# DeltaNet and a PReLU feed-forward on one core: the opening of the kernel put in another order

## The chip, the core and the metric

The kernel runs on one core of a Trainium2 chip. Its engines work side by side, each through its own queue of instructions in the order written: TensorE (PE, with its weight loads shown as PEld), VectorE (DVE), ScalarE (ACT), GpSimd (POOL) and SyncE (SP, which here only starts DMAs). They wait for each other by semaphores. The time is device microseconds of the whole program, as a median over runs.

## The reference

There are 4 batches of 8 heads, 768 tokens each, head dimension 48. For every head a 48x48 state goes through the tokens:

```python
k_n = k / (np.linalg.norm(k, axis=-1, keepdims=True) + 1e-06)
for t in range(S):
    y[:, :, t] = einsum('bhd,bhde->bhe', q[:, :, t], state)
    v_old = einsum('bhde,bhd->bhe', state, k_n[:, :, t])
    state = state + beta[t] * einsum('bhd,bhe->bhde', k_n[:, :, t], v[:, :, t] - v_old)
```

The 3072 outputs of 384 numbers (8 heads x 48) then go through a feed-forward: `h = x @ w_in` (384 x 2048), `g = max(h, 0) + alpha * min(h, 0)` with one alpha for each of the 2048 columns, and `g @ w_out` (2048 x 384). All is float32.

## The kernel before

**Tiling.** The recurrence is cut into 12 chunks of 64 tokens. A step is one chunk of two batches: one batch in partitions 0 to 63, the other in 64 to 127, so there are N = 24 steps and 8 heads in each. Inside a chunk the recurrence is a triangular system of 64 unknowns for each head and batch. Its matrix is the Gram matrix of the keys, weighted by beta and the keys' norms. It is inverted by blocks: 32x32 diagonal blocks first, and what lies between them by products.

**What one step needs.** `squared` squares the keys on ACT (L348). `norms` sums them on DVE (L352). `weigh` takes the root and adds the epsilon on ACT (L364, L365); its second half, `weigh_rest`, takes the reciprocal on DVE (L371), and multiplies beta and the weights by it on POOL (L373, L374). `flip` transposes the keys on PE (L384), and an ACT copy brings them to SBUF as `k_t` (L410, or L393 in `flipped`). `grams` makes the Gram matrix on PE (L436). It returns three pieces, which are called later: two DVE evictions that apply the weights (L442, into `same` and `right`), and `keep`, which copies one part of `right` into `same` on POOL (L485), DVE (L487) or ACT (L489).

**The first four steps** (NJ = 4) are inverted together, since their diagonal blocks fill the 128 lanes. `turn_in` puts the blocks one to a lane by four DVE transposes (L501). `eliminate_small` inverts the 16x16 sub-blocks on the diagonal: a product with a mask `inside` (L563), then 14 steps of two DVE instructions each (L569, L575), while POOL clears the rest of the tile (L580 to L582). `back` transposes the result into the tiles `turned` and `inverse` (L501). `cross` then joins the 16x16 blocks to 32x32 ones on PE: products of `edge` and `turned` (L605), a copy on ACT to `half_way` (L610), products with `half_way` for `turned` (L615) and for `inverse` (L622), and DVE additions of both (L629, L631). `place` puts the blocks into `diag` and `inv` (L650, L654), and `between_1` (L721) and `between_2` (L734) join them to 64x64.

**Order.** Every engine's order is written out by hand; nothing is reordered. The main body first issues all loads on SP, makes the four steps' Gram matrices in a loop, transposes the queries of steps 0 and 1 (`flips(N, i)`, copies L412), makes the products of queries and keys (`queries`, L1417), transposes alpha (`slopes`, L310, and on ACT L311 into `al_t`), clears tiles on ACT (`zeros`, L327 and L329), and calls `busy(BUSY)`: products of 128x512 that nobody reads (L1407), each shown as two records in the trace. `begin_in(4)` puts the first ACT halves of the weights' conversion on ACT's queue (L226, L227; the DVE halves are L236 and L241). Then come the elimination, `first_chunk` (steps 0 and 1 as far as the state), and `second_pair`, where steps 2 and 3 go along with the first feed-forward products (L943). From there a planner (`weave`) mixes the pieces of recurrence and feed-forward by their counts.

PSUM tiles: `ps_big` and `ps_one` go round three pairs of banks, `ps_ffn` round two single banks.

## Time and profile before

| | us |
|---|---|
| time, median of 3 runs | 661.9 (661.86 to 667.46) |
| span of the profiled execution, first to last instruction | 658.5 |
| median less span | 3.4 |
| PE busy | 642.4 (98%) |
| DVE busy | 490.4 (74%) |
| ACT busy | 263.9 (40%) |
| POOL busy | 93.4 (14%) |
| PE busy in the first 22 us | 13.7 |

The profile gives the profiled execution's span, and no other time of its own; the 3.4 us are the median's distance from that span.

How to read it: in the timeline a line has the start and the length in microseconds, engine, line of the kernel, operation, what is written and read, and how many instructions were merged. In square brackets stands the idle time of that engine just before it, and what ended that. In the chain of work that ended last each line has a start, a length, and an engine with the tile and line; "issue" is time for which the profile shows no one that was waited for. A line number can be that of a helper, which several callers share.

### The profile page before, as it was taken

To read this page: it belongs to the slowest core of one execution; us is meant where nothing else is said; L and a number is where in the kernel's file an instruction comes from. 1 tells how busy PE (TensorE), PEld (TensorE's weight loads), DVE (VectorE), ACT (ScalarE), POOL (GpSimd) and SP (SyncE) were. 2 spreads that over 40 slices of the span, in tenths; PEclk is the share of its full clock that TensorE was granted. 3 is DMA by queue.
4 is the path that set the end of the run, shared out by engine and by line. 5 is a ranking of instruction groups with operands and counts; after the bars stand their busy time and mean duration, and the time that the engine had idled before them with its cause. 6 is when DMAs were issued, how large, how long until landed. Compare 5 with 4: busy or idle time off the path is not lost.

```text
span 658.5 us, 22123 instructions
## 1 busy us (share of the span) xinstructions
PE 642.4 (98%) x9545; PEld 567.5 (86%) x9545; DVE 490.4 (74%) x1180; ACT 263.9 (40%) x621; POOL 93.4 (14%) x201
## 2 busy tenths in 40 slices
PE   5999999999999999999999999999999999999997
PEld 4477888657788988988988988988989999999997
DVE  3975899977999779658869758868868658567383
ACT  4855755344453443143253242133245245042140
POOL 6000211010000000000000000000035044052260
PEclk9999999999999999999999999999999999999999
DMA  7946745311422122122111111111111210100000
GB/s 124 293 97 158 194 121 148 73 36 37 75 54 50 34 54 38 25 59 41 26 43 33 26 39 36 26 42 33 26 44 32 45 32 2 31 8 2 24 1 25
DMA packets 111154, 37.72 MB, mean 57 GB/s; under 512 B 104224, under 2 KB 107440, under 8 KB 111056
## 3 DMA queue, kind: packets, MB, share of 16 engines
q1 hardware_dynamic: 109184, 35.81, 24.5%
q8 instruction: 75, 1.23, 0.8%
q10 hardware_dynamic: 1872, 0.49, 0.4%
q14 instruction: 23, 0.19, 0.1%
HBM read 31.56 MB, written 4.72 MB: 55 GB/s over the span
## 4 chain that ended last, share of the span: by engine, by line
PE 91%; DVE 5%; ACT 1%; issue 1%; POOL 1%; DMA 1%; SPq 0%; POOLq 0%; ACTq 0%; DVEq 0%
PE p_ffn L943 24%; PE p_ffn L1008 17%; PE p_more L1260 8%; PE p_ffn L986 5%; PE p_more L1176 5%; PE p_ffn L1166 3%; PE p_ffn L1260 3%; PE p_pair L775 2%; PE p_pair L384 2%; PE p_ffn L1171 2%; PE p_pair L686 2%; PE p_pair L800 2%; PE p_pair L813 2%; PE p_pair L1407 2%; PE p_pair L436 2%; PE p_pair L760 1%
## 5 line engine op out<-in xcount | busy, mean ns | idle before, releaser
L943 PE MATMUL p_ffn<-xt,w_in 128*128 128x256 f32 x768 | 176.1, 383 | 0.6 <-DVE act L955 0.5
L943 PEld LDWEIGHTS p_ffn<-xt,w_in 128*128 128x128 f32 x768 | 142.4, 190 | 21.2 <-issue 1.5
L955 DVE SCALAR_TENSOR_TENSOR act<-act,al_t,p_ffn 128x256 f32<-128x256 f32 x112 | 48.7, 476 | 26.5 <-ACT act L953 26.5
L953 ACT ACTIVATE act<-p_ffn 128x512 f32<-128x512 f32 x56 | 33.2, 594 | 79.4 <-PE p_ffn L943 79.2
L534 DVE TENSOR_TENSOR block<-block,prod 128x30 f32<-128x30 f32 (+9 forms) x150 | 49.8, 332 | 5.2
L1200 POOL TENSOR_TENSOR k_t<-k_t 128x128 f32<-128x128 f32 (+1 forms) x48 | 29.3, 610 | 167.1 <-ACT k_t L1195 164.6
L528 DVE TENSOR_TENSOR prod<-block 128x30 f32<-128x30 f32 (+9 forms) x150 | 48.8, 326 | 1.4
L1008 PE MATMUL p_ffn<-w_out,act 128*128 128x192 f32 x288 | 49.6, 328 | 0.0
L854 ACT COPY xt<-p_pair 128x384 f32<-128x384 f32 x22 | 10.4, 478 | 91.1 <-PE p_pair L852 77.3
L1008 PEld LDWEIGHTS p_ffn<-w_out,act 128*128 128x128 f32 x288 | 46.5, 190 | 0.3
L373 POOL TENSOR_TENSOR beta_t<-beta_t,rec 128x8 f32<-128x8 f32 x24 | 6.3, 265 | 283.9 <-DVE rec L371 268.6
L1200 POOL TENSOR_TENSOR block<-block 128x128 f32<-128x128 f32 (+1 forms) x48 | 27.9, 582 | 17.2 <-ACT block L1195 14.7
L1166 PE MATMUL p_ffn<-xt,w_in 128*128 128x256 f32 x96 | 28.7, 381 | 0.5 <-DVE o_sb L1028 0.5
L785 DVE TENSOR_TENSOR r<-v_raw,p_pair 64x192 f32<-64x192 f32 (+1 forms) x66 | 23.3, 353 | 2.3 <-PE p_pair L775 1.2
L698 ACT COPY inv<-p_pair 32x256 f32<-32x256 f32 x40 | 14.4, 361 | 25.0 <-DVE u L804 24.2
L352 DVE TENSOR_REDUCE norm<-ksq 128x8 f32<-128x384 f32 x24 | 13.0, 548 | 14.3 <-ACT ksq L348 14.3
L804 DVE TENSOR_TENSOR u<-p_pair,wgt 128x384 f32<-128x384 f32 x24 | 13.2, 556 | 14.0 <-PE p_pair L686 14.0
L1028 DVE TENSOR_TENSOR o_sb<-u,p_ffn 128x192 f32<-128x192 f32 x24 | 8.0, 352 | 20.4 <-PE p_ffn L1008 20.0
L1214 DVE SCALAR_TENSOR_TENSOR act<-block,al_t,act 128x256 f32<-128x256 f32 x32 | 19.1, 638 | 5.3 <-ACT block L1210 5.2
L764 ACT COPY y<-p_pair 128x384 f32<-128x384 f32 x22 | 10.4, 478 | 30.2 <-PE p_pair L760 26.1
L1260 PE MATMUL p_more<-w_out,act 128*128 128x192 f32 x128 | 21.8, 329 | 0.0
L1195 ACT COPY k_t<-p_more 128x512 f32<-128x512 f32 x16 | 9.4, 585 | 31.1 <-PE p_more L1176 26.4
(228 smaller groups left out, 1422.1 us busy)
## 6 DMA issues: line engine op xcount, KB each, us to landing
w_out<-in_moe_w_in_dram SPq DMA_DIRECT2D x10, 512.0 KB, 5.5
qp<-in_q_dram SPq DMA_DIRECT2D x48, 96.0 KB, 3.0
v_raw<-in_v_dram SPq DMA_DIRECT2D x48, 96.0 KB, 2.9
kl<-in_k_dram SPq DMA_DIRECT2D x96, 48.0 KB, 2.5
out_dram<-o_sb SPq DMA_DIRECT2D x90, 48.0 KB, 1.6
space_out<-in_moe_w_out_dram SPq DMA_DIRECT2D x11, 384.0 KB, 4.1
ke<-in_k_dram SPq DMA_DIRECT2D x43, 96.0 KB, 3.3
w_out<-in_moe_w_out_dram SPq DMA_DIRECT2D x5, 384.0 KB, 4.0
```

The lines of the kernel that those rows point to most:

```text
L528: nc.vector.tensor_tensor(out=prod, in0=r[:, 0:j, j : j + 1].to_broadcast([128, j, n]), in1=r[:, j : j + 1, j + 1 : HB].to_broadcast([128, ...
L534: nc.vector.tensor_tensor(out=r[:, 0:j, j + 1 : HB], in0=r[:, 0:j, j + 1 : HB], in1=prod, op=ALU.add)
L785: nc.vector.tensor_tensor(out=r[to, a], in0=v_in[to, a], in1=p[own, a, :, 0:D], op=ALU.subtract)
L943: nc.tensor.matmul(p_h[:, i], w_in[:, t, (f + i) * 128 : (f + i + 1) * 128], xt[:, t], start=(t == 0), stop=(t == KT - 1),)
L953: nc.scalar.activation(g, p_h, ACT.Relu, scale=-1.0)
L955: nc.vector.scalar_tensor_tensor(out=g[:, i], in0=g[:, i], scalar=al_t[:, f + i : f + i + 1], in1=p_h[:, i], op0=ALU.mult, op1=ALU.add,)
L986: nc.tensor.matmul(p_o[u], gs[f // 2][:, f % 2, u * 128 : (u + 1) * 128], w_out[:, f], start=(f == 0), stop=(f == FT - 1),)
L1008: nc.tensor.matmul(p, x(i), w(i), start=(i == 0), stop=(i == FP - 1))
L1166: nc.tensor.matmul(p[:, f * 256 : f * 256 + 256], w(2, f), xt[:, 2], start=True, stop=False)
L1176: nc.tensor.matmul(q[:, j], a, b, start=True, stop=True)
L1200: nc.gpsimd.tensor_tensor(out=dst, in0=a, in1=b, op=ALU.add)
L1260: nc.tensor.matmul(p, x(i), w(i), start=(i == 0), stop=(i == FP - 1))
```

## The change

The opening's order is written anew, and four things beside it are altered:

- All four steps' norms, reciprocals and weights are put ahead of the evictions of the Gram matrices as far as possible, in the queues of ACT, DVE and POOL; the POOL copies of `keep` come after the weights. For steps 2 and 3 `keep` uses DVE and ACT and no longer POOL. The transposed keys use the two single banks.
- The mask `inside` with its tile `ones` and its cast on ACT is gone. In its place 15 POOL memsets clear what lies below the diagonal.
- `slopes` comes after the queries.
- `cross` adds the products for `turned` (L629) ahead of the products for `inverse` (L622), with a `yield` between them. `first_chunk` places the first parts of `diag` in that gap, and its filler `busy(1.25)` is gone.
- `BUSY` is 6 instead of 8 (12 records instead of 16), and 6 products of the identity with itself (128x128) stand at PE's beginning.

```diff
-BUSY = 8
+BUSY = 6
+WARM = 6
...
-    ones = work.tile([128, HB, HB], FP32, name="ones", tag="turned", bufs=1)
-    nc.gpsimd.memset(ones, 0.0)
-    nc.gpsimd.affine_select(
...
@@ keep
-            if n < FIRST + NJ and n != NJ - 1:
+            if n < 2 or NJ <= n < FIRST + NJ:
                 nc.gpsimd.tensor_copy(out=same[m][own, j], in_=right[n % EARLY][own, 1:])
@@ eliminate_small
-        nc.vector.tensor_tensor(out=x, in0=x, in1=own_blocks(inside_), op=ALU.mult)
+        for j in range(1, LB):
+            nc.gpsimd.memset(x[:, :, j, 0:j], 0.0)
@@ cross
+        for i in (0, 2):
+            y = turned[m][quad(i), bs, 0:LB]
+            nc.vector.tensor_tensor(out=y, in0=y, in1=p[quad(i), 1], op=ALU.add)
+        yield
         for b in range(n):
             for i in range(4):
                 nc.tensor.matmul(
...
-        for i in (0, 2):
-            y = turned[m][quad(i), bs, 0:LB]
-            nc.vector.tensor_tensor(out=y, in0=y, in1=p[quad(i), 1], op=ALU.add)
@@ first_chunk
         next(middle)
-        busy(1.25)
         place(0, (0,))
         place(1, (0,), True)
+        next(middle)
         for i in both:
             place(i, (1,), True)
+        for i in both:
             now(between_1(i))
@@ main body
-    squares(0)
-    flips(0, N)
+    for _ in range(WARM):
+        nc.tensor.matmul(big[0][:, 0, 0:128], ident, ident)
+    squared(0)
+    norms(0)
+    now(flipped(0, ps_ffn()))
+    squared(1)
+    norms(1)
     betas()
     fetch_in(n_in + 2)
-    squares(1)
-    now(weigh(0))
-    for n in range(1, NJ):
-        if n == 1:
-            gram = grams(0)
-        flips(n, N)
-        if n > 1:
-            gram = grams(n - 1)
-        now(gram)
-        if n + 1 < NJ:
-            squares(n + 1)
-        now(weigh(n))
-        load_early(n + NKE)
-    now(grams(NJ - 1))
-    nc.scalar.copy(inside, ones)
+    rest = [weigh(0), weigh(1)]
+    gram = {0: grams(0)}
+    squared(2)
+    now(flipped(1, ps_ffn()))
+    for x in rest:
+        now(x)
+    norms(2)
+    rest = weigh(2)
+    now(flipped(2, ps_ffn()))
+    squared(3)
+    now(rest)
+    now(gram[0][:2])
+    load_early(1 + NKE)
+    gram[1] = grams(1)
+    norms(3)
+    rest = weigh(3)
+    now(flipped(3, ps_ffn()))
+    now(rest)
+    now(gram[1][:2])
+    for n in range(2, NJ):
+        load_early(n + NKE)
+        gram[n] = grams(n)
+    for n in range(2, NJ):
+        now(gram[n - 2][2:])
+        now(gram[n][:2])
+    for n in range(2, NJ):
+        now(gram[n][2:])
+    for i in range(2):
+        flips(N, i)
     edges(0, edge)
     load_late(1)
     load_v(2)
-    slopes()
-    for i in range(2):
-        flips(N, i)
     for i in range(2):
         load_q(i + 2)
     mask = queries()
+    slopes()
@@ second_pair
         next(halves[0])
+        next(halves[0])
...
         next(halves[1])
+        next(halves[1])
```

More of the change, by code (lines that the diff above doesn't have):

```diff
@@ L265 @@
         nc.gpsimd.tensor_copy(out=above[half(t)], in_=upper[half(t), half(t)])
-    ones = work.tile([128, HB, HB], FP32, name="ones", tag="turned", bufs=1)
-    nc.gpsimd.memset(ones, 0.0)
-    nc.gpsimd.affine_select(
-        out=ones, in_=ones, compare_op=ALU.is_ge, fill=1.0, base=0,
-        pattern=[[1, HB], [-1, HB]], channel_multiplier=0,
-    )
-    inside_ = const.tile([128, HB * (HB + 1)], S8, name="inside")
-    inside = inside_[:, 0 : HB * HB].rearrange("p (r c) -> p r c", c=HB)
     which = const.tile([128, 2], FP32, name="which")
@@ L438, in grams @@
             )
-        w = stats[n][1][:, 0:2, :, None].to_broadcast([128, 2, G, HB])
         def weighted(dst, cols):
+            w = stats[n][1][:, 0:2, :, None].to_broadcast([128, 2, G, HB])
             nc.vector.tensor_tensor(
```

## The prediction

> **What bounds the kernel now.** I read three views: the busy times by stretch of the span, the chain that ended last in its order of time, and the timeline of each engine up to 62 us.

> The stretches (length; busy time and count of PE, PEld, DVE, ACT, POOL; clock; DMA share; GB/s):

> ```profile
> 0.00:22.00 22.00, 13.66 (x224) 11.20 (x225) 11.51 (x35) 11.87 (x36) 10.93 (x43) 1.00 0.82 190
> 22.00:41.60 19.60, 18.97 (x416) 11.02 (x414) 15.78 (x46) 13.11 (x28) 0.00 (x0) 1.00 0.80 198
> 54.00:100.00 46.00, 45.59 (x973) 38.95 (x974) 36.82 (x97) 31.57 (x73) 8.63 (x20) 1.00 0.62 159
> ```

> After 54 us PE is never free; the longest PE waits there that name another engine are 0.5 us. So the end is about the time at which PE reaches 54 us, plus 604.5. Only the opening can move it, and a microsecond saved before 54 should be one at the end. Only 3.4 us lie outside the span (661.9 median less 658.5); I have no other own time of the profiled execution.

> The chain in the opening (start, length, what):

> ```profile
> 12.29 0.39 POOL same L485
> ...
> 13.20 0.21 POOL beta_t L373
> ...
> 16.03 0.42 DVE same L442
> 16.45 0.34 DVE right L442
> 16.81 0.41 ACT same L489
> 17.25 1.03 ACT inside L1553
> 18.29 0.62 ACT sums L589
> ...
> 19.51 1.98 PE p_ffn L1417 x57
> 21.49 9.26 PE p_pair L1407 x16
> 30.75 1.32 PE p_pair L605 x88
> ```

> GpSimd copies (L485) stand ahead of the next step's weights (L373), the cast of the mask stands ahead of the query copies, and then 16 fillers hold PE until 30.7. The timeline shows what else is late (start, length, instruction, idle before and its releaser):

> ```profile
> 15.74 0.28 PE L310 MATMUL p_pair<-ident,al_sb 16*128 16x16 f32 x1 [1.68 <-DMA al_sb<-in_moe_alpha_dram]
> 19.63 0.69 DVE L563 TENSOR_TENSOR block<-block,inside 128x512 f32<-128x512 f32 x1
> 20.38 0.15 POOL L582 MEMSET block<- 128x32 f32 x1 [0.24 <-DVE block L563]
> 24.99 0.34 PEld L1407 LDWEIGHTS p_pair<-kl,ident 128*128 128x128 f32 x1 [0.52 <-issue]
> 26.30 0.19 PEld L1407 LDWEIGHTS p_pair<-kl,ident 128*128 128x128 f32 x1 [0.24 <-issue]
> 32.34 0.37 ACT L610 COPY act<-p_pair 128x256 f32<-128x256 f32 x1 [1.26 <-PE p_pair L605]
> 36.97 0.84 DVE L629 TENSOR_TENSOR turned<-turned,p_pair 32x256 f32<-32x256 f32 x2 [1.41 <-PE p_pair L622]
> ```

> The fillers come every 0.85 us until 25.85 and every 0.43 after: TensorE doubles its rate there, though the clock column says 1.00 throughout.

> **A. Grams and weights.** DVE's order changes. norm 1 (L352) goes ahead of the four betas (spacing 0.265): betas end near 8.2, reciprocals 0 and 1 near 8.4 and 8.6, norm 2 at 9.15. Root and add on ACT end at 9.74, reciprocal 2 at 9.97, the pair of evictions of gram 0 at 10.73, norm 3 at 11.27, reciprocal 3 at 11.96, gram 1's pair at 12.7. GpSimd makes each weight 0.5 after its reciprocal, with no copy ahead of it. PE: transposes 1 and 2 end at 9.65 as now, gram 1 (1.13) at 10.75, transposes 3 (1.07) at 11.8, its copy on ACT at 12.4, gram 2 at 12.9, gram 3 at 14.0. So PE comes last: gram 3's evictions end at 14.8, two DVE copies of 0.28 and one on ACT at 15.3, and L501 begins at 15.3, not 17.25: **1.95 earlier**. The loads moved on SP cost nothing: SP issues without a stall to 18.5, and the same six ke loads follow.

> **B. Clears for the product.** L563 goes: 0.69, and about 0.04 of issue. Fifteen memsets come on GpSimd, idle at that time. The nearest rows are 0.09 (32x1) to 0.15 (128x32), so some 2 us beside 7.9 us of elimination, whose reads lie above the diagonal. If every step had to wait for them it would cost 2.0; L582 at 20.38 ran beside L569 (0.19, as long as its equal at 27.72, 0.20), so I take 0. The first step starts at 15.3 + 2.28 + 0.1 = 17.7 instead of 20.36.

> [...]

> **C. ACT.** The cast (1.05) goes. The slopes' transpose no longer holds up PE for alpha's DMA (1.68), so the query transposes run from 14.0 to 16.0; their second copy ends at 16.6, the queries (1.98) at 18.6, the slopes (0.28) at 18.9. But `al_t` on ACT now waits behind the queries, and the clears behind `al_t`. `minus` starts at 19.05 instead of 19.82. From there to the end of the first eight conversions ACT is full for 11.27 us (19.82 to 31.09): free at **30.3**.

> **D. Fillers.** Twelve from 18.9: with the doubling 4.4 after their start as now, 5 x 0.854 + 7 x 0.43 = 7.3, so 26.2. `turned` is ready at 17.7 + 7.91 + 1.09 = 26.7 (steps and two transposes: 20.36 to 28.27, then 1.09). L605 then ends at 28.1, and its copy L610 must wait for ACT: 30.33 instead of 32.34, **2.0 earlier**. ACT, not PE, is late next; doubling up to 2.4 later is hidden under it. Six warm-ups of a quarter filler (0.43) fit between `ident` (1.47) and the first keys (4.42): 0, up to 0.3 if they overrun, which the wait for beta at 5.79 hides.

> **E. Crossing.** L610 to the first L721 took 6.07 (32.34 to 38.41). Now L629 waits for L615 only: L610 to L615 0.72, L615 with its fillers and L622 3.86 (33.06 to 36.92), then L721: 30.33 + 0.72 + 3.86 + 0.04 = 34.95, **3.46 earlier**. The cover holds: L615 ends at 32.97; DVE's own work ends at 17.7 + 15.2 = 32.9 (20.36 to 35.56); L629 ends at 33.84 and ACT's L654 at 34.4, under L622. The dropped 1.25 filler costs nothing, since PE has L721. In `second_pair` DVE's order stays the same: 0.

> **F. What arrives.** From L721 to 54 us all waits are on PE, ACT and DVE work that moves along, except idle time put down to issue (0.42 at 39.53, 0.20 at 44.05, 1.59 at 52.32). If those end at dates of their own, up to all the gain is lost there; if they go, 2.2 more comes. I take them as moving along, since none names a transfer. Sum: 658.5 - 3.4 = 655.1 of span, **658.5 us** of time.

> **Rivals.**
> 1. *The warm-ups double the rate at once.* Transposes take 0.65 and grams 0.6; DVE is then last in A, L501 starts at 14.65, the queries take 1.25, L610 could start at 28.6, and DVE is free at 32.2: L721 at 33.65, 4.75 earlier, **657.1**. Against: from 5.83 to 14.07 PE had no gap above 0.36 and stayed slow (2.01 for eight transposes at 15.95). For: the rise came under 128-row fillers, which the warm-ups resemble. [...]
> 2. *The issue gap at 52.32 ends at its own date.* PE then waits longer: 660.5 if half is lost, 661.9 if all.
> 3. *Slower: the rate falls back.* If rival 1 comes true, the fillers end at 22.3 and L605 waits until 26: 3.7 us with PE empty. The trace has no fall in a 1.59 gap, none longer after the rise. If the rate halves there, no unbroken stretch raises it before 54. PE's path from 30.7 to 54 is about 20 us of small matmuls; 64 of them took 1.99 before the rise and 1.15 (L813) after, so +60%, 12 us: 657.1 + 12 = **669**. It decides from the first L605 on.
> 4. *PE waits for L629 before L622*, as they share a tile. In `second_pair` L629 comes on DVE at 60.68, 2.5 after L615, twice about 3 us: 661.9 - 3.4 + 0.9 + 6 = 665.4. Against: L580 ran while L563 wrote other columns of the same tile, and L721 ran beside L650.

> **Numbers.** Forecast 0.45, rival 1 0.20, rival 2 0.17, rival 3 0.06, rival 4 0.06, more than 1% gained by vanishing gaps 0.06. Forecast, rivals 1 and 2 with vanishing gaps partly and the memsets' full price give 655.5 to 662; the before runs themselves reach 667.46, so I set the upper end at 664.5. 1% (6.6 us) is about what a measurement of this kernel can tell from no change: faster 0.06; slower 0.07 (rival 3 and a little of 4); same 0.87.

> **What would show it.** Right: L501 near 15.3, first L569 near 17.7, `minus` near 19.1, an ACT wait at `al_t`, L610 right after a conversion near 30.3, L721 near 35, and the second-pair L605 near 48.2 with its gap. Wrong: a doubled rate before 20 us; L569 waiting on GpSimd; L622 waiting on DVE; idle time to issue that grew by what was saved.

## The result, and the profile after

The changed kernel takes **667.64 us** (median of 14 runs, 665.88 to 669.44) against 661.88 (14 runs, 659.25 to 668.58): 1.0071 times as long, 95% interval 1.0043 to 1.0098. I had forecast 658.5 and a range to 664.5. The ratios in this document are taken over undisturbed runs alone: runs of the kernel before that lie more than 1.5% above its fastest, all of them with a mean granted clock of TensorE of 0.985 or less (experiment 8), are left out, so a ratio can differ from the quotient of two medians. The profiled execution of the changed kernel took 668.38 us, 666.7 of it span, 8.2 more than the span before. The medians lie only 5.8 apart: by its span the profiled execution before took about 660.2 us (an estimate; time and span of a run differ by 1.7), 1.7 less than its kernel's median, and the one after took 0.7 more than its own.

The page's row of the granted clock (the share of full speed that TensorE was given, in tenths), in 40 slices of 16.7 us:

```profile
PEclk9859999999999999999999999999999999999999
```

The page's average hides the first slices' detail, so the next view is of stretches (length; busy time and count of PE, PEld, DVE, ACT, POOL; clock; DMA share; GB/s):

```profile
17.00:23.20 6.20, 6.16 (x60) 2.85 (x49) 5.53 (x21) 5.96 (x20) 1.40 (x18) 1.00 0.99 387
23.20:27.30 4.10, 0.00 (x0) 0.00 (x0) 3.65 (x14) 3.93 (x10) 0.00 (x0) 0.96 1.03 402
27.30:51.40 24.10, 23.62 (x593) 19.39 (x593) 14.43 (x33) 9.48 (x20) 0.00 (x0) 0.51 0.49 87
60.00:72.00 12.00, 8.32 (x212) 6.78 (x212) 5.82 (x19) 6.30 (x16) 0.95 (x4) 0.86 0.59 158
```

TensorE is empty from 23.2 to 27.3, and for the 24 us behind that its clock is half (0.51). From 60 to 72 it stands idle again, and the clock sags to 0.86. The timeline shows the instructions (lines have moved: L492 was L501, L561 was L569, L597 was L605, L607 was L615, L614 was L629, L618 was L622, L714 was L721, L727 was L734, L1400 was L1407). First VectorE, GpSimd and ScalarE in the opening (start, busy time, engine, line; in brackets the idle time ahead and what ended it):

```profile
15.91 2.29 DVE L492 STREAM_TRANSPOSE block<-same 128x256 f32<-128x256 f32 x4
17.80 0.89 POOL L555 MEMSET block<- 128x2 f32 x15 [2.69 <-DVE block L492]
17.93 0.25 ACT L1574 ACTIVATE minus<-above 128x64 f32<-128x64 f32 x1
18.23 0.19 DVE L561 TENSOR_TENSOR prod<-block 128x28 f32<-128x28 f32 x1
```

Then PE, through the first pair and the crossings of the second:

```profile
14.30 1.95 PE L376 MATMUL p_pair<-ident,qp 128*112 128x128 f32 x8
...
16.35 1.30 PE L1410 MATMUL p_ffn<-beside,k_t 48*64 48x64 f32 x64
17.75 5.42 PE L1400 MATMUL p_pair<-kl,ident 128*128 128x512 f32 x12
27.35 1.90 PE L597 MATMUL p_pair<-turned,sums 32*32 32x16 f32 x128 [4.19 <-DVE turned L492]
...
35.43 1.91 PE L618 MATMUL p_pair<-inverse,act 32*32 32x16 f32 x128
...
42.53 3.52 PE L727 MATMUL p_pair<-diag,mid 64*64 64x32 f32 x62
...
63.90 0.74 PE L618 MATMUL p_pair<-inverse,act 32*32 32x16 f32 x64 [2.88 <-DVE turned L614]
64.57 1.10 PE L376 MATMUL p_pair<-ident,qp 128*112 128x128 f32 x4
65.46 3.97 PE L936 MATMUL p_ffn<-xt,w_in 128*128 128x256 f32 x12
...
70.84 0.73 PE L618 MATMUL p_pair<-inverse,act 32*32 32x16 f32 x64 [0.81 <-DVE turned L614]
```

The queries take 1.30 us instead of 1.98 and the twelve filler records 5.42, so the rate rose while the queries ran, from 16.35 on. Then comes an idle time of 4.19, and behind it everything is slow: 1.91 for the products of `inverse` (1.38 before), 3.52 for 62 of `between_2` (2.00 before). In the second pair TensorE waits 2.88 and 0.81 us for VectorE's additions (L614); the transposes behind the first wait take 1.10 instead of 0.65. The same work before the change:

```profile
30.68 1.39 PE L605 MATMUL p_pair<-turned,sums 32*32 32x16 f32 x128
...
35.54 1.38 PE L622 MATMUL p_pair<-inverse,act 32*32 32x16 f32 x128
...
41.58 2.00 PE L734 MATMUL p_pair<-diag,mid 64*64 64x32 f32 x62
...
53.91 0.71 PE L605 MATMUL p_pair<-turned,sums 32*32 32x16 f32 x62 [1.59 <-issue]
...
58.89 0.65 PE L384 MATMUL p_pair<-ident,qp 128*112 128x128 f32 x4
```

Where the 8.2 us come from, by the start of the same work on PE in both traces:

| work | before | after | difference |
|---|---|---|---|
| first filler | 21.42 | 17.75 | -3.67 |
| first product of the crossing | 30.68 | 27.35 | -3.33 |
| first product of `between_1` | 38.41 | 37.26 | -1.15 |
| `between_2` | 41.58 | 42.53 | +0.95 |
| first product of the second pair's crossing | 51.57 | 55.73 | +4.16 |
| its first run of ten feed-forward products | 55.47 | 58.09 | +2.62 |
| feed-forward products behind its crossings | 63.27 | 71.50 | +8.23 |
| end | 658.5 | 666.7 | +8.2 |

So the fillers start 3.7 us earlier. From there to the second pair's crossing 7.8 are lost: the hole and the half rate behind it, less what the split and the dropped filler of the first crossing save. A gap put down to issue (1.59 before) went and gave 1.5 back, and the second pair's two waits, with the slower work behind the first, took 5.6.

### The profile page after: what moved, and what is told of

Same layout as the page of the kernel before. It is cut to its first block, busy times and chain, and to the rows that moved or that the text cites. A ratio compares the mean times of both kernels' runs of the same rounds, so it can differ in the third digit from the quotient of the medians.

```text
span 666.7 us, 22130 instructions
## 1 busy us (share of the span) xinstructions
PE 650.7 (98%) x9549; PEld 576.2 (86%) x9549; DVE 491.3 (74%) x1180; ACT 264.1 (40%) x621; POOL 90.7 (14%) x212
## 4 chain that ended last, share of the span: by engine, by line
PE 88%; DVE 5%; DMA 2%; ACT 2%; SPq 2%; issue 1%; ACTq 0%; DVEq 0%
PE p_ffn L936 23%; PE p_ffn L1001 17%; PE p_more L1253 8%; PE p_ffn L979 5%; PE p_more L1169 4%; PE p_ffn L1159 3%; PE p_ffn L1253 3%; PE p_pair L376 2%; PE p_pair L768 2%; PE p_ffn L1164 2%; PE p_pair L679 2%; PE p_pair L806 2%; PE p_pair L793 2%; PE p_pair L428 1%; PE p_pair L753 1%; DMA space_out<-in_moe_w_in_dram 1%
## 5 line engine op out<-in xcount | busy, mean ns | idle before, releaser
L344 DVE TENSOR_REDUCE norm<-ksq 128x8 f32<-128x384 f32 x24 | 12.9, 545 | 12.7 <-ACT ksq L340 12.7
L1188 ACT COPY k_t<-p_more 128x512 f32<-128x512 f32 x16 | 9.4, 586 | 31.4 <-PE p_more L1169 26.7
```

## The experiments

Theory W: the second pair's loss is TensorE waiting for VectorE's additions. Theory C: the middle loss is the rate of TensorE, which falls in an idle time that the faster opening creates. The ratios below compare with runs of the kernel before on the same chip.

**1. The second pair's crossings joined again.** In `second_pair` both additions come behind all products, as before the change. `add_turned` holds the two additions of L614.

```diff
@@ cross
+        if not joined:
+            add_turned()
+            yield
...
+        if joined:
+            add_turned()
@@ second_pair
-        halves = [cross(0, slice(i * H, i * H + H), edge, half_way) for i in both]
+        halves = [cross(0, slice(i * H, i * H + H), edge, half_way, None, True) for i in both]
...
         next(halves[0])
-        next(halves[0])
...
-        next(halves[1])
```

> The changed kernel with one part undone: in the second pair both additions of a crossing come behind all its products again, as before the change; the first crossing stays split. Theory W (in the second pair TensorE waits before the products for `inverse` until VectorE has added to `turned`: 2.88 and 0.81 us of idle time in the trace, and 5.6 us from the first feed-forward products behind the crossing's first half, 2.6 late, to those behind its end, 8.2 late): those 5.6 us go, 667.6 falls to 662. Rival (the loss there is the lower rate of TensorE carried on, or VectorE's backlog, which the order of the additions does not change): 667.6 stays, within 1.5.

Measured: 662.41 us (10 runs), ratio 0.9968 (0.9925 to 1.0011). The 5.2 us are gone, and the profile names no engine that TensorE waits for there. The half rate stays (mean clock 0.974 to 0.985 over the runs): the other loss is untouched, and W holds.

**2. The split kept, the products in two PSUM tiles.**

```diff
-        p = ps_big()[:, :, 0 : n * LB].rearrange("p w (b i) -> p w b i", i=LB)
+        p, p_i = (
+            ps_one()[:, 0 : n * LB].rearrange("p (b i) -> p b i", i=LB) for _ in range(2)
+        )
...
```

> The changed kernel with the split kept everywhere, but the products for `turned` and those for `inverse` in two PSUM tiles of their own instead of the two halves of one. If the wait of theory W comes only from the two sharing a tile, the idle time before the products for `inverse` in the second pair goes, and the time falls by as much as with the joined crossing: 662. If the wait has another reason (the matrices read, VectorE's queue), it stays: 667.6.

Measured: 662.15 us, ratio 0.9982 (0.9934 to 1.0030). The products for `inverse` now follow those for `turned` at once. The timeline of PE:

```profile
57.94 0.64 PE L609 MATMUL p_pair<-act,inverse 32*32 32x16 f32 x29
...
58.46 0.71 PE L620 MATMUL p_pair<-inverse,act 32*32 32x16 f32 x62
59.10 0.65 PE L376 MATMUL p_pair<-ident,qp 128*112 128x128 f32 x4
```

So the wait comes from the shared tile: in the changed kernel the products for one half of a PSUM tile wait 2.88 and 0.81 us for VectorE's additions, which read the other half and stand before them in the program; with two tiles the profile shows no wait of TensorE from 50 to 75 us.

**3. Eight fillers instead of six.**

```diff
-BUSY = 6
+BUSY = 8
```

> The changed kernel with 8 fillers of 512 again (16 records instead of 12), all else as changed. Theory C (the rate of TensorE rises early, the fillers end at 23.2, TensorE is empty for 4.2 us until the crossing at 27.35, and the rate falls back in that hole until 51): the hole shrinks to about 2.4 us, the rate stays up, and most of what was lost from 27 to 55 us comes back: some 8 us, 660. If a hole of 2.4 us is enough for a fall, or if the rate falls for another reason: 667.6.

Measured: 667.28 us, ratio 1.0065 (1.0028 to 1.0101): missed. The timeline of PE shows why:

```profile
26.29 1.25 PE L597 MATMUL p_pair<-turned,sums 32*32 32x16 f32 x128 [2.49 <-DVE turned L492]
...
33.30 1.90 PE L618 MATMUL p_pair<-inverse,act 32*32 32x16 f32 x128 [2.23 <-DVE turned L614]
```

And the stretches of the same run:

```profile
26.20:31.00 4.80, 4.71 (x198) 3.24 (x198) 4.80 (x12) 4.52 (x8) 0.00 (x0) 1.00 1.08 179
31.00:33.30 2.30, 0.07 (x1) 0.03 (x1) 2.22 (x7) 0.11 (x1) 0.00 (x0) 0.83 0.39 65
33.30:50.00 16.70, 15.74 (x396) 14.39 (x397) 7.56 (x17) 4.82 (x12) 0.00 (x0) 0.51 0.41 89
```

The rate outlives the hole of 2.49 us (clock 1.00 until 31). But now TensorE is early in the first crossing too, waits 2.23 us for L614 there, and the rate falls in that wait (0.83 on average over it, 0.51 behind it). The shared tile costs in the first crossing as well, as soon as TensorE is fast.

**4. Without the warm-up products** (WARM = 0; they feed nothing).

> The changed kernel without the 6 products of the identity with itself at TensorE's beginning (they feed nothing). If these raise the rate early: it now rises inside the fillers, the 12 records take about 7.3 us from 18.5 instead of 5.4, they end near 26, there is no hole, and the small products from 27 to 51 us run at the full rate: about 660.5. If the early rise is only chance of phase, as many runs as before have the hole: 667.6.

Measured: 671.92 us (10 runs), ratio 1.0123 (1.0074 to 1.0173): missed, and the wrong way. The timeline:

```profile
11.83 1.44 PE L428 MATMUL p_pair<-k_t 48*64 48x64 f32 x64
13.20 1.09 PE L376 MATMUL p_pair<-ident,qp 128*112 128x128 f32 x8
...
26.50 1.90 PE L597 MATMUL p_pair<-turned,sums 32*32 32x16 f32 x128 [4.53 <-DVE turned L492]
```

The rate is up at 13 us (eight transposes in 1.09) with no warm-up. In the new opening they are not needed for the early rise. They may bring it earlier: in the traces of experiments 1, 2 and 3 the first 32 Gram products take 0.69 us at 7.31, 6.55 and 7.25 us, against 1.13 in the changed kernel and in this run, but later ones are slow again there (32 Gram products in 1.13 us at 9.26 in experiment 1 and in 1.14 at 9.20 in experiment 3, eight transposes in 1.95 at 12.82 in experiment 2). Why the median without them is 4 us above the changed kernel's, though the profile has a span of 666.1, I can't say.

**5. Two tiles and ten fillers.** BUSY = 10 on top of experiment 2.

> The changed kernel with two PSUM tiles in the crossing (as in the run of the products apart, 662.2) and 10 fillers of 512 (20 records) instead of 6. Theory C: the fillers end at about 25.2, a microsecond before the crossing, there is no other hole of 2 us until 50, so TensorE keeps its full rate in every run (mean clock 0.995 and more instead of 0.98), the second pair begins some 6.4 us earlier than with 6 fillers: 656, better than both kernels. If the rate falls for another reason than the hole, or the fillers hold TensorE back as much as they save: 661 to 662.

Measured: 661.28 us, ratio 1.0022 (0.9995 to 1.0049), mean clock 0.979 to 0.990: the rate still falls, now elsewhere.

```profile
34.56 0.77 PE L716 MATMUL p_pair<-diag,right 64*64 64x32 f32 x19
37.11 2.66 PE L716 MATMUL p_pair<-diag,right 64*64 64x32 f32 x45 [1.78 <-issue]
```

The stretches of the same run, in the columns named above:

```profile
28.50:35.30 6.80, 6.80 (x346) 5.17 (x345) 5.28 (x14) 3.57 (x7) 0.00 (x0) 1.00 0.69 93
35.30:37.10 1.80, 0.02 (x1) 0.00 (x0) 1.73 (x5) 0.00 (x0) 0.00 (x0) 0.67 0.31 48
37.10:50.00 12.90, 12.89 (x251) 11.79 (x252) 5.52 (x13) 4.57 (x11) 0.00 (x0) 0.52 0.46 107
```

Inside the products of `between_1` TensorE stands still for 1.78 us, put down to issue; up to there the clock is 1.00, behind it 0.52.

**6. The kernel before with the second pair's split alone.**

> The kernel before the change with one part of it alone: in the second pair both crossings are split as in the change (the two halves of one PSUM tile). Theory W: TensorE waits for VectorE twice there, some 5.6 us: where the clock stays up, 667.5 instead of 662. Rival (the split costs only in company with the late opening, when VectorE lags behind): 662, within 1.5.

Measured: 669.87 us (8 runs), beside 664.45 for the kernel before on that chip; ratio 1.0048 (0.9962 to 1.0133), so by all runs unclear. The expectation was for runs in which the clock stays up: three runs have a mean clock of 0.994 or more and a median of 665.0 us, against 659.5 for the eight such runs of the kernel before on that chip, 5.5 more, as W has it. The timeline, of a run of 675.19 us, shows the waits of the changed kernel in the old opening:

```profile
69.37 1.05 PE L631 MATMUL p_pair<-inverse,act 32*32 32x16 f32 x64 [2.87 <-DVE turned L624]
...
77.58 0.59 PE L631 MATMUL p_pair<-inverse,act 32*32 32x16 f32 x50 [0.68 <-DVE turned L624]
```

**7. The shared tile with ten fillers.** BUSY = 10, nothing else.

> The changed kernel with 10 fillers, the PSUM tile shared as changed. The hole before the first product of the crossing goes, but with a fast TensorE the wait for VectorE's addition inside the first crossing (2.23 us with 8 fillers) stays. If that second hole is enough to lose the rate, as with 8 fillers: 667, mean clock 0.98. If the rate was lost with 8 fillers through the first hole (2.5 us) and the second together: the rate holds, mean clock 0.99 and more, and 656 + 5.6 = 661.5.

Measured: 668.72 us (4 runs), ratio 1.0156 (1.0074 to 1.0238), mean clock 0.982 to 0.987. The hole before the crossing is down to 0.92 us, but the 2.07 us of waiting for L614 inside it and 1.50 us put down to issue stay, and so does the half rate (3.52 us for 62 products of `between_2`, 2.00 before the change).

**8. The kernel before once more.**

> The kernel before the change once more, for a second profile. Its 31 timed runs lie in two groups: mean clock 0.99 to 1.00 with 658.5 to 665, and 0.982 to 0.99 with 667 to 673. Theory C: in the second group the rate of TensorE falls back between 30 and 55 us as in the changed kernel; a profile with a clock of 0.985 shows the crossing's products at the half rate (L605 1.9 us instead of 1.4), one of 1.00 does not.

One run, 663.64 us, mean clock 0.994, which lies between the two groups. Its timeline:

```profile
34.03 0.37 PE L605 MATMUL p_pair<-turned,sums 32*32 32x16 f32 x22 [1.96 <-issue]
35.38 0.68 PE L615 MATMUL p_pair<-act,inverse 32*32 32x16 f32 x32
36.83 1.04 PE L615 MATMUL p_pair<-act,inverse 32*32 32x16 f32 x32
```

It stands still for 1.96 us inside the first products of the crossing, and soon after the same 32 products take 1.04 instead of 0.68. So the kernel before can lose the rate in the same place, and does so more rarely than the changed one. Over its 90 runs beside the experiments that I pooled (1, 5, 9 and 11), 45 have a mean clock of 0.995 or more (median 660.7 us) and 34 one of 0.99 or less (669.5). All 14 runs of the changed kernel have 0.985 or less.

**9. Two tiles, nine fillers, and three held back.** The last three stand between the crossing and `between_1`.

```diff
         next(middle)
+        busy(3, pause[0])
         for i in both:
             place(i, (1,), True)
```

> The changed kernel with two PSUM tiles in the crossing, 9 fillers of 512 before it and 3 (6 records, about 2.6 us) behind its last product, ahead of the first product of the 64x64 blocks. Theory C, widened: with 10 fillers the rate still fell, in a hole of 1.78 us inside those products (35.3 to 37.1, put down to issue), which ended at 37.1 to 37.6 in the three runs with the earliest crossing. If that hole ends at a date of its own, the new fillers cover it at no cost, the rate holds (mean clock 0.995 and more), and the second pair begins 4 us earlier than with 10 fillers: 657. Rival: the hole comes a fixed time after the instructions before it, so that it only moves behind the new fillers: they cost 2.6 us and the rate falls all the same, 663 to 664, mean clock 0.98.

Measured: 659.81 us (10 runs, 657.60 to 662.92), ratio 0.9954 (0.9904 to 1.0003), mean clock 0.984 to 0.997. The stall inside `between_1` is gone, but the rate falls earlier and returns under the held fillers:

```profile
26.39 1.35 PE L597 MATMUL p_pair<-turned,sums 32*32 32x16 f32 x128 [1.88 <-DVE turned L492]
...
35.76 5.44 PE L1402 MATMUL p_pair<-kl,ident 128*128 128x512 f32 x6
41.12 2.06 PE L716 MATMUL p_pair<-diag,right 64*64 64x32 f32 x64
```

Its stretches:

```profile
26.40:41.00 14.60, 14.60 (x332) 8.25 (x332) 9.29 (x22) 4.70 (x9) 0.00 (x0) 0.53 0.79 143
41.00:54.00 13.00, 12.53 (x351) 10.35 (x350) 8.42 (x18) 8.38 (x17) 0.00 (x0) 1.00 0.32 84
```

**10. All crossings joined, eight fillers:** the new order, the clears and the warm-ups alone, with the filler of 1.25 back.

> The changed kernel with all crossings joined as before the change (with the filler of 1.25 behind the first) and 8 fillers of 512: what is left of the change is the opening's order, the clears in place of the product, and the warm-ups. If the order is worth what its instructions show (the crossing begins about 3 us earlier) and the rate holds: 659, mean clock 0.995 and more. If the rate falls here too, because the earlier crossing meets the holes put down to issue: 663 to 665, mean clock 0.98.

Measured: 663.26 us, ratio 0.9999 (0.9958 to 1.0039), mean clock 0.977 to 0.991: the pessimistic case. The crossing begins at 26.20 instead of 30.68, a stall of 0.89 us put down to issue stands in it from 31.4 to 32.3, and behind it the small products are slow: 3.52 us for 62 of `between_2` (2.00 before the change), and still 1.80 for 64 of L813 at 47.27 (1.15 before). So the new order by itself brought nothing on the whole.

**11 and 12. Eleven fillers and three held back; twelve and four.**

> As the run with 9 fillers and 3 held back, but with 11 fillers before the crossing. There the rate fell in a hole of 1.88 us just ahead of the crossing, and came back at about 41 us under the held fillers. Theory C: with 4 more records (1.7 us) that hole is 0.2, the rate holds from 16 us on (mean clock 0.995 and more), the products from 29 to 41 us save some 4 us: 656, below both kernels. Rival (the rate falls whatever stands in TensorE's queue, at the next stall put down to issue): 660 to 661, mean clock 0.985 to 0.99.

> The same with 12 fillers before the crossing and 4 held back: 4 records more, 1.7 us at the full rate. Theory C: if 11 and 3 still leave a hole, this has none, mean clock 0.995 and more; each record that covers no hole costs 0.43 on TensorE: 657 to 658. Rival: the rate falls all the same, and the fillers cost their own time: 662.

Measured: 658.88 us (12 runs, 657.83 to 662.81; mean clock 0.989 to 0.997), ratio 0.9973 (0.9941 to 1.0005), and 661.89 us, ratio 0.9981 (0.9937 to 1.0026). The first has the lowest median of all here, 2.8 below that of all runs of the kernel before on that chip, but the interval still holds 1, so that it beats the kernel before isn't shown. Its timeline:

```profile
27.32 1.26 PE L597 MATMUL p_pair<-turned,sums 32*32 32x16 f32 x128
...
32.94 1.22 PE L620 MATMUL p_pair<-inverse,act 32*32 32x16 f32 x111 [0.57 <-issue]
34.09 4.52 PE L1402 MATMUL p_pair<-kl,ident 128*128 128x512 f32 x6
38.54 2.06 PE L716 MATMUL p_pair<-diag,right 64*64 64x32 f32 x64
```

And the stretch that holds the whole crossing and the held fillers:

```profile
27.30:38.50 11.20, 10.63 (x333) 6.25 (x332) 8.87 (x22) 5.04 (x9) 0.00 (x0) 0.85 0.76 118
```

The crossing begins 3.4 us earlier than before the change (27.32 to 30.68), and `between_1` at the same time as before (38.54 to 38.41): the held fillers eat the gain, in part at the half rate (4.52 us for records that take 0.43 each at the full one). What I expected of it, 656, would have needed the rate and no fillers in the way.

## Why the prediction was wrong

**Where it went wrong, in short:** section D put TensorE's rise too late and so saw no hole behind the fillers, and E put the split of the second pair at 0.

**A and B were right in kind.** L501 starts at 15.91 (15.3 worked out, 17.25 before): beta arrived 0.74 later in this run, and the betas with it. The first elimination step comes at 18.23 (17.7 worked out), the clears take 0.89 us rather than 2 and delay no step: the first four instructions of the elimination, from 18.23 on, take 0.19, 0.19, 0.21 and 0.21, as before.

**C** was right in its order and too late in its times: `minus` at 17.93 instead of 19.05, for the most part since the queries ran at the doubled rate.

**D failed first.** I took "with the doubling 4.4 after their start as now", and the rate was up before them. That is rival 1 in its effect on the queries (1.25 worked out, 1.30 measured) and the fillers (end at 22.3 worked out, 23.2 measured), which I gave 0.20. It is not rival 1 in its start: the rate did not double at once, and the eight transposes from 14.30 on still took 1.95 us. The hole is rival 3's, and rival 3 came too: 3.7 us empty worked out, 4.19 measured, 12 us of lost time worked out, 7.8 measured from the first filler to the second pair. Its price was too high because the 60% came from two unlike products (L436 and L813); the path from the first crossing to the second pair's went from 20.9 us to 28.4, 36% more. That nothing would raise the rate again before 54 us was an estimate; it came back at 50.84. I had argued against rival 1 with a row of the old, sparser opening ("PE had no gap above 0.36 and stayed slow"), and had treated 1 and 3 as separate small chances. What brings the rise was not shown: experiment 4 is fast at 13 us without a warm-up (eight transposes in 1.09), the kernel before slow until 25.85. But 3 follows from 1, and 12 fillers at 0.43 in front of an elimination that ends at a fixed time left the hole for certain.

**E failed on its cover.** "PE has L721" after the crossing was true, but L618 waited for L614, hidden in the changed kernel only by the slow fillers around it, and shown in the open by experiments 3 and 7.

**"In `second_pair` DVE's order stays the same: 0"** was the second wrong step, and rival 4 was right: 2.88 and 0.81 us of waiting plus the slowed work behind it, 5.6 in all where I had 6 (5.2 and 5.5 by experiments 1 and 2, 5.5 by experiment 6). My rows against it, L580 beside L563 and L721 beside L650, were SBUF tiles; none showed a PSUM tile that is read in one half and written in the other.

**F** held for the tail: from 72 us on nothing changes (+8.23 and +8.2). The gap at 52.32 went in this run, so rival 2 did not come true as it was put. But experiments 5, 7 and 10 show stalls put down to issue in new places once PE is early, and in the traces of experiments 3, 5 and 7 the products of `between_1` go on only at 37.1 to 37.6, as if at a date of their own; in experiments 1, 2 and 10 they do not, so this isn't shown.

The two losses, 7.8 and 5.6, against gains of 3.7 and 1.5 give the 8.2 us of span, and moved the time out of my range. One reading of mine was also off: the 3.4 us that I put outside the span. Each run on record with both numbers has its time 1.7 to 1.8 us above its span (668.38 and 666.7), so about half of the 3.4 was the distance between the profiled execution and the median.

**When the rate falls.** The size of a hole alone does not decide it: the rate held through 2.49 us in experiment 3, and fell inside the holes of 1.78 (experiment 5) and 2.23 us (experiment 3), 2.3 us behind the one of 1.96 (experiment 8), and in experiment 11 with none above 0.57 in front. The traces show a pattern that orders these cases. Stretches of the changed kernel between the changes of its clock, then single ones of experiment 3 (the first two) and 11:

```profile
26.95:50.84 23.89, 23.11 (x591) 19.12 (x591) 14.26 (x33) 9.34 (x19) 0.00 (x0) 0.50 0.50 90
50.84:64.50 13.66, 10.62 (x328) 8.57 (x324) 7.39 (x17) 8.49 (x18) 0.48 (x2) 1.00 0.60 158
64.50:67.91 3.41, 3.41 (x24) 2.92 (x13) 0.79 (x3) 2.14 (x6) 0.48 (x2) 0.50 0.19 34
```

```profile
22.27:25.69 3.42, 1.52 (x4) 0.38 (x2) 2.97 (x13) 3.30 (x8) 0.00 (x0) 1.00 1.02 412
29.10:32.51 3.41, 1.97 (x44) 1.18 (x37) 3.38 (x10) 1.69 (x3) 0.00 (x0) 1.00 0.60 93
30.68:34.09 3.41, 2.84 (x164) 2.23 (x163) 3.33 (x9) 1.47 (x3) 0.00 (x0) 1.00 0.55 95
```

**What stays open.** How much work, and of which shape, keeps the rate from one mark to the next was not measured: in the second group, TensorE was busy for 1.52 us with fillers alone and kept it, and for 1.97 and 2.84 us with fillers and small products mixed, and lost it. That the marks alone make the two groups of the kernel before is an inference; no run of its slower group left a trace. What the stalls put down to issue are was not tried.

## What to carry to other kernels

When an opening gets faster, ask what will be empty at the new times: fillers that were sized for a slow TensorE end early on a fast one (here 5.42 us for twelve records, 7.3 worked out), and the hole behind them can cost more than the opening gained (here 7.8 us against 3.7). Before splitting a group of products so that one half is read early, put the halves in PSUM tiles of their own, for the products for one half may wait for the read of the other (2.88 and 0.81 us here). And a rival that follows from another one is no separate small chance; price the two as one path.

## What was not expected of the hardware

- The clock fell inside holes of 1.78 us (experiment 5) and 2.23 us (experiment 3) next to small products, held through one of 2.49 us behind fillers (experiment 3), and its changes in the changed kernel lie 23.89, 13.66 and 3.41 us apart, multiples of 3.41. In the changed kernel the half rate then lasted 24 us, although TensorE was busy for nearly all of it (23.62 of 24.10 us): for most of that time small products did not bring it back, while in experiments 9 and 11 it came back under six records of 512 columns (5.44 and 4.52 us).
- The products were fast at 13 us with no warm-up (experiment 4: eight transposes in 1.09 us), in the queries from 16.35 on in the changed kernel (1.30 us instead of 1.98), and from 25.85 before the change (fillers 0.43 us apart instead of 0.85). In experiments 1 to 3, with the warm-ups, 32 Gram products were already fast at 6.55 to 7.31 us (0.69 instead of 1.13), and later ones slow again.
- Fifteen small clears on GpSimd took 0.89 us together, 0.06 each, less than the 0.09 of the nearest row.
